# Regrouping the last stage of batch 0, splitting a table load, and moving three closing stores in a fused Fourier-filter and MLP kernel

## Chip, cores, metric

The kernel runs on one core of a Trainium2 chip. Times are device microseconds (us). "Time" is what is measured from outside; the profile's "span" runs from the first to the last instruction on the core and is about 1.8 us shorter. PE is TensorE's matmul stream, PEld its weight loads, DVE is VectorE, ACT ScalarE, POOL GpSimd, SP SyncE. An engine's name with a q is its sequencer.

## The reference

```python
# x: (8, 3008, 256)   filt_r, filt_i: (1505, 256)
X = np.fft.rfft(x, axis=1)
y = np.fft.irfft(X * (filt_r + 1j * filt_i)[None], n=3008, axis=1)
h = y.reshape(24064, 256) @ w_in                  # (256, 2048)
g = h + np.sin(alpha * h)**2 / (alpha + 1e-09)
out = g @ w_out                                   # (24064, 256), float32
```

## The kernel before

The Fourier transforms are done as small matmuls: 3008 points are 94 x 32, so each transform is one stage over 94 and one over 32. Batch 0 has a path of its own, kept in SBUF, on the chip; its last stage turns `t4_0` into `y`, the input of the hidden layer. Everything after that is a stream: for each chunk of 512 columns, 16 hidden blocks (two matmuls, a sine on ACT, a combination on DVE) and then the output projection, with the transforms of the next batches put between them at fixed slots.

Three places matter here. The first is the load of the inverse table `e_t`, in two halves on POOL's queue, each behind four loads of the filter:

```python
for g in range(2):
    gs = slice(12 * g, 12 * g + 12)
    for k, filt in enumerate((filt_r, filt_i)):
        for q in range(2):
            ...                                       # a quarter of this half of the filter
            nc.gpsimd.dma_start(out=f_t[k][64*k + 32*q : ..., gs, :], in_=...)
    nc.gpsimd.dma_start(out=e_t[:, gs, :], in_=e_dram.ap()[:, gs])
```

The second is the last stage of batch 0, in groups of four row columns. A pair of groups (one for each half of the channels) goes through a pool of two PSUM buffers, where the results of matmuls lie; ACT evacuates the first group (copies it to SBUF), DVE the second:

```python
def last(self, u, on_act=None):
    ch, rest = divmod(u, 4); half, cb = divmod(rest, 2)
    n0 = 8 * ch + 4 * half
    ps = fps.tile([128, 4, 128], FP32, tag="f")
    ...                                               # 4 x 2 matmuls into psv
    evac(y[:, cb, self.b % 2, n0:n0 + 4, :], psv, on_act)

def last_two(self, u):
    self.last(u, True)
    self.last(u + 1, False)
...
s0.last(0, True); s0.last(2, True); s0.last(1, True); s0.last(3, False)   # ahead of the hidden layer
for u in range(4, 16, 2):
    put((1, 3, 4.5, 6, 14, 16)[u // 2 - 2], s0.last_two, u, pe=True)      # inside the stream
```

The third is the output. A block of 128 rows is stored in runs, since rows of `out` lie 32 apart; each run is one DMA. All go to SP, except that the short second runs of the very last chunk go to POOL (first two tiles of 128 rows) and to ACT (last two tiles):

```python
store(o[:, i, :], pb, c0 + 128 * (t - t % 2 + i),
      nc.scalar if final else nc.gpsimd if k == len(chunks) - 1 else nc.sync)
```

## Time and profile before

| | before |
|---|---|
| time, median of the first 3 runs | 789.39 us (788.52 to 789.53) |
| span of the profiled run (its time: 790.81 us) | 789.0 us |
| first transpose of batch 0's inverse | 30.38 |
| first hidden block, from its second matmul (the first ran at 36.08) | 36.79 |
| end of the last matmul | 784.80 |
| SP's last store issued | 786.57 |

PE is busy 98% of the span. What the change touches is the first 55 us, where PE waits, and the 4.2 us after the last matmul. The lines that show this are in the prediction.

### The profile page before, as it was taken

Reading aid. Unit: us, or ns where it says so; the run is one execution under the profiler, and the core shown is the slowest. Engines: PE = TensorE matmul, PEld = TensorE weight load, DVE = VectorE, ACT = ScalarE, POOL = GpSimd, SP = SyncE. Lnnn points to the kernel's source line nnn. Section 1 sums busy time; section 2 is a strip of 40 time slices with the busy share of each in tenths; the row PEclk is TensorE's granted clock in tenths of the full one; section 3 lists DMA queues with packets and bytes.
Section 4 is the critical chain, followed back from the end, with each engine's and each line's share of the span. In section 5 each row is a group of like instructions: output and inputs, shape, how many; then the busy total and the mean of one; then the engine's idle time right before and its main releaser. Section 6 shows DMA issues by size and latency. Waiting matters only on the chain.

```text
span 789.0 us, 16730 instructions
## 1 busy us (share of the span) xinstructions
PE 776.2 (98%) x5854; PEld 536.3 (68%) x5854; DVE 657.4 (83%) x1171; ACT 617.0 (78%) x1209; POOL 79.7 (10%) x125
## 2 busy tenths in 40 slices
PE   8999989999999999999999999999999999999997
PEld 4756757676667766777666766777666776766666
DVE  7887987899878997799978998799987999777773
ACT  6887868888878887888887888788887887777663
POOL 6442000200020000200020000200002000000000
PEclk9999999999999999999999999999999999999999
DMA  9956568755573646554575455845566233421111
GB/s 217 257 105 173 118 144 206 173 104 134 140 198 82 135 98 191 150 121 102 121 210 124 100 106 137 219 94 113 128 165 171 62 97 82 116 62 29 41 41 54
DMA packets 87677, 101.01 MB, mean 128 GB/s; under 512 B 14472, under 2 KB 75928, under 8 KB 87592
## 3 DMA queue, kind: packets, MB, share of 16 engines
q1 hardware_dynamic: 78016, 73.73, 34.5%
q0 software_dynamic: 9360, 26.15, 17.4%
q8 instruction: 46, 0.75, 0.4%
q14 instruction: 39, 0.32, 0.1%
q10 hardware_dynamic: 216, 0.05, 0.0%
HBM read 55.72 MB, written 46.66 MB: 130 GB/s over the span
## 4 chain that ended last, share of the span: by engine, by line
PE 90%; DVE 2%; DMA 2%; ACT 2%; issue 1%; POOL 1%; SPq 1%; ACTq 0%; POOLq 0%; DVEq 0%
PE po L523 40%; PE ph L507 40%; PE pa L180 3%; PE pd L258 2%; PE pb L200 2%; PE pc L231 2%; DMA e_t<-e_tbl 1%; DVE v L511 1%; PE pd L255 1%; DMA xs<-xf 1%; ACT cos_all L510 1%; DVE t_h L385 1%; SPq L549 1%; ACT t_h L159 1%; DVE t_h L161 0%
## 5 line engine op out<-in xcount | busy, mean ns | idle before, releaser
L511 DVE SCALAR_TENSOR_TENSOR v<-cos_all,ph 128x512 f16<-128x512 f32 (+1 forms) x768 | 482.8, 671 | 107.4 <-ACT cos_all L510 103.9
L510 ACT ACTIVATE cos_all<-ph 128x512 f32<-128x512 f32 (+1 forms) x768 | 410.9, 592 | 99.5 <-PE ph L507 98.3
L523 PE MATMUL po<-w,v 128*128 128x256 f16 x3008 | 388.7, 272 | 0.0
L507 PE MATMUL ph<-y,w 128*128 128x512 f16 (+1 forms) x1536 | 386.4, 374 | 0.5 <-DVE y L161 0.3
L523 PEld LDWEIGHTS <-v 128*128 128x128 f16 x3008 | 289.3, 98 | 78.2 <-issue 1.2
L507 PEld LDWEIGHTS <-w 128*128 128x128 f16 x1536 | 147.5, 98 | 104.5 <-issue 2.5
L529 ACT COPY o<-po 128x512 f32<-128x512 f32 (+1 forms) x97 | 55.6, 573 | 19.6 <-PE po L523 12.6
L203 ACT CAST xf<-pb 128x512 f16<-128x512 f32 x84 | 50.0, 595 | 15.2 <-PE pb L200 13.8
L192 POOL DMA_DIRECT2D t<-d x56 | 36.3, 666 | 202.4 <-DMA out_dram<-o 128.6
L159 ACT CAST t_h<-pa 96x512 f16<-96x512 f32 x74 | 43.3, 586 | 8.5 <-PE pa L180 8.3
L140 POOL DMA_DIRECT2D x<-in_x_dram x32 | 17.1, 535 | 302.1 <-PE pc L231 171.4
L159 ACT CAST y<-pd 128x376 f16<-128x376 f32 x83 | 40.0, 482 | 7.6 <-PE pd L258 5.3
L258 PEld LDWEIGHTS <-t_h 96*128 96x128 f16 x448 | 31.4, 97 | 18.4 <-issue 0.4
L180 PE MATMUL pa<-x,wf_t 94*96 94x512 f16 x112 | 42.2, 381 | 1.0 <-DVE t_h L161 0.6
L159 ACT CAST g<-pc 128x512 f16<-128x512 f32 x58 | 34.4, 593 | 9.4 <-PE pc L231 9.0
L221 DVE TENSOR_TENSOR p<-p,xs 128x512 f16<-128x512 f16 x84 | 35.7, 425 | 2.9
L220 DVE TENSOR_TENSOR xs<-xs,filt_t 128x512 f16<-128x512 f16 x84 | 35.0, 416 | 2.8 <-DMA xs<-xf 2.8
L258 PE MATMUL pd<-wi_t,t_h 96*128 96x94 f16 x448 | 37.1, 204 | 0.0
L214 DVE TENSOR_TENSOR p<-xf,filt_t 128x512 f16<-128x512 f16 x84 | 35.0, 416 | 0.0
L231 PE MATMUL pc<-p,e_t 128*128 128x256 f16 x168 | 32.1, 273 | 1.7 <-DVE p L221 1.7
L200 PE MATMUL pb<-t,d_t 128*128 128x256 f16 x168 | 32.1, 272 | 0.5 <-DVE g L161 0.4
L161 DVE CAST t_h<-pa 96x512 f16<-96x512 f32 x38 | 25.9, 681 | 0.7 <-PE pa L180 0.5
(66 smaller groups left out, 257.5 us busy)
## 6 DMA issues: line engine op xcount, KB each, us to landing
x<-in_x_dram POOLq DMA_DIRECT2D x30, 376.0 KB, 5.0
d<-t_h SPq DMA_DIRECT2D x28, 384.0 KB
t<-d POOLq DMA_DIRECT2D x56, 192.0 KB, 4.6
xs<-xf SPq DMA_DIRECT2D x168, 64.0 KB
d<-g SPq DMA_DIRECT2D x56, 192.0 KB
t_h<-d SPq DMA_DIRECT2D x28, 384.0 KB
out_dram<-o SPq DMA_DIRECT2D x104, 80.0 KB
w_out<-in_moe_w_out_dram SPq DMA_DIRECT2D x1, 2048.0 KB
```

The source lines that it names most:

```text
L159: marks["act"] = nc.scalar.copy(out=dst, in_=src)
L180: marks["pe"] = nc.tensor.matmul(out=ps[0:NK, :], lhsT=wf_t, rhs=self.x[ch][:, 2 * j:2 * j + 2, :], start=True, stop=True)
L192: nc.gpsimd.dma_start(out=self.t2[g][64 * p:64 * p + 64, :, :], in_=self.d1[a0:a0 + 6, :, :].rearrange("s n c -> n s c"))
L200: nc.tensor.matmul(out=ps[:, i, :], lhsT=d_t[:, s, :], rhs=self.t2[s // 6][:, s % 6, :], start=True, stop=True)
L203: nc.scalar.copy(out=self.xf[u], in_=ps)
L231: nc.tensor.matmul(out=ps[:, i, :], lhsT=e_t[:, 2 * w + i, :], rhs=pt[:, i, :], start=(k == 0), stop=(k == len(pr) - 1))
L258: nc.tensor.matmul(out=psv[:, i, :], rhs=wi_t, start=True, stop=True, lhsT=t4_h[ch // 2][0:NK, n0 % 16 + i, cb * 128:cb * 128 + 128])
L507: nc.tensor.matmul(out=ps[:, 0:n], lhsT=w1[:, cb, jb * 128:jb * 128 + 128], rhs=y_cols[:, cb, c0:c0 + n], start=(cb == 0), stop=(cb == 1))
L510: nc.scalar.activation(out=cs[:, 0:n], in_=ps[:, 0:n], func=AFT.Sin, bias=float(np.pi / 2))
L511: marks["snake"] = nc.vector.scalar_tensor_tensor(out=v[k][:, jb, 0:n], in0=cs[:, 0:n], scalar=-1.0, in1=ps[:, 0:n], op0=ALU.add, op1=ALU. ...
L523: nc.tensor.matmul(out=pso[k][:, t % 2, :], lhsT=v[k][:, jb, 128 * t:128 * t + 128], rhs=w2[:, jb, :], start=(jb == 0), stop=(jb == 15))
L529: nc.scalar.copy(out=o[:, i0:t % 2 + 1, :], in_=pso[k][:, i0:t % 2 + 1, :])
```

## The change

Its intent: the first inverse matmuls waited for the table, so its first four classes are loaded apart, ahead of the filter's imaginary rows (A). The first hidden chunk needs only six row columns of the last stage, so the groups ahead of it have three each and the later ones five and four, and both groups of a pair go to one engine, the pairs alternating between DVE and ACT (B). And three more stores of the last chunk go from SP to POOL (C; not named in the change's title). Unused code that goes with it is cut.

```diff
+            if (g, k) == (0, 1):
+                nc.gpsimd.dma_start(out=e_t[:, 0:4, :], in_=e_dram.ap()[:, 0:4])
...
-        nc.gpsimd.dma_start(out=e_t[:, gs, :], in_=e_dram.ap()[:, gs])
+        es = slice(4 if g == 0 else 12, 12 * g + 12)
+        nc.gpsimd.dma_start(out=e_t[:, es, :], in_=e_dram.ap()[:, es])
...
+    def last_0(cb, n0, n1, on_act):
+        ...                                   # the same matmuls for row columns n0 to n1
+        evac(y[:, cb, 0, n0:n1, :], psv, on_act)
+    def last_two(i, n0, n1):
+        last_0(0, n0, n1, ([i % 2 == 1] * 2)[0])
+        last_0(1, n0, n1, ([i % 2 == 1] * 2)[1])
...
-    s0.last(0, True)
-    s0.last(2, True)
+    last_0(0, 0, 3, True)
+    last_0(0, 3, 6, True)
     warm_pe(3)
-    s0.last(1, True)
-    s0.last(3, False)
+    last_0(1, 0, 3, True)
+    last_0(1, 3, 6, False)
...
-                      nc.scalar if final else nc.gpsimd if k == len(chunks) - 1 else nc.sync)
+                      *(nc.sync, nc.scalar) if final else (nc.gpsimd if i else nc.sync, nc.gpsimd)
+                      if k == len(chunks) - 1 else (nc.sync, nc.sync))
...
-    for u in range(4, 16, 2):
-        put((1,3,4.5,6,14,16)[u // 2 - 2], s0.last_two, u, pe=True)
+    for i, n0 in enumerate((6, 11, 16, 20, 24, 28)):
+        put((1,3,4.5,6,14,16)[i], last_two, i, n0, (11, 16, 20, 24, 28, 32)[i], pe=True)
```

More of the change, by code (lines that the diff above doesn't have):

```diff
@@ L244, in load_t4, with last @@
                                in_=self.d2_rows[:, 8 * ch:8 * ch + 8, :])
-        def last(self, u, on_act=None):
+        def last(self, u):
             ch, rest = divmod(u, 4)
@@ L252, in last @@
             for i in range(4):
-                if self.b == 0:
-                    for k in range(2):
-                        nc.tensor.matmul(out=psv[64 * k:64 * k + 64, i, :], lhsT=t4_0[cb][:, n0 + i, :, k],
-                                         rhs=wi0_t, start=True, stop=True)
-                else:
-                    nc.tensor.matmul(out=psv[:, i, :], rhs=wi_t, start=True, stop=True,
-                                     lhsT=t4_h[ch // 2][0:NK, n0 % 16 + i, cb * 128:cb * 128 + 128])
-            evac(y[:, cb, self.b % 2, n0:n0 + 4, :], psv, on_act)
-        def last_two(self, u):
-            self.last(u, True)
-            self.last(u + 1, False)
+                nc.tensor.matmul(out=psv[:, i, :], rhs=wi_t, start=True, stop=True,
+                                 lhsT=t4_h[ch // 2][0:NK, n0 % 16 + i, cb * 128:cb * 128 + 128])
+            evac(y[:, cb, self.b % 2, n0:n0 + 4, :], psv)
     warm = cpool.tile([128, 1], FP32)
@@ L425, in inverse_0 @@
         evac(g_0[hc][:, 4 * w:4 * w + 4], ps.rearrange("p s (k c) -> p s c k", k=2), not (i in ()))
+    def last_0(cb, n0, n1, on_act):
+        ps = fps.tile([128, 4, 128], FP32, name=f"pd_0_{cb}_{n0}", tag="f")
+        psv = ps.rearrange("p a b -> p (a b)")[:, 0:(n1 - n0) * NR].rearrange("p (a r) -> p a r", r=NR)
+        for n in range(n0, n1):
+            for k in range(2):
+                nc.tensor.matmul(out=psv[64 * k:64 * k + 64, n - n0, :], lhsT=t4_0[cb][:, n, :, k],
+                                 rhs=wi0_t, start=True, stop=True)
+        evac(y[:, cb, 0, n0:n1, :], psv, on_act)
+    def last_two(i, n0, n1):
+        last_0(0, n0, n1, ([i % 2 == 1] * 2)[0])
+        last_0(1, n0, n1, ([i % 2 == 1] * 2)[1])
     w1 = cpool.tile([128, 2, DFF], FP16)
@@ L452, in weights_in @@
             after(ins, marks["products"])
-    s0 = Spectral(0)
     [inverse_table(g) for g in range(2)]
@@ L537, in runs, with store @@
         return [(0, whole), (whole, cnt - whole)] if 0 < whole < cnt else [(0, cnt)]
-    def store(o_blk, pb, col, second):
+    def store(o_blk, pb, col, *queues):
         p = 0
-        queues = [nc.sync, second]
         while p < 128:
```

## The prediction

> **What bounds the kernel now.** I read the page first, then the chain that ended last from 17 to 50 us, then the timeline of single engines there and over the last 11 us.
>
> ```profile
> span 789.0 us, 16730 instructions
> PE 776.2 (98%) x5854; PEld 536.3 (68%) x5854; DVE 657.4 (83%) x1171; ACT 617.0 (78%) x1209; POOL 79.7 (10%) x125
> ```
>
> PE is busy for 98%. The two large groups of matmuls are untouched, so the change can only win PE's idle time: at the start, in the first chunk, and after the last matmul. The chain shows the start (start us, us, what):
>
> ```profile
> 11.77 9.71 DMA e_t<-e_tbl
> 21.48 0.05 issue
> 21.53 0.64 PE pc L422 x8
> ...
> 30.38 4.51 DVE t_h L385 x2
> 34.89 0.04 issue
> 34.94 1.23 PE pd L255 x16
> 36.16 0.02 issue
> 36.19 0.56 DVE y L161
> 36.75 0.05 issue
> 36.79 0.82 PE ph L507 x3
> ```
>
> The first inverse matmuls wait until 21.48 for the inverse table; two transposes on DVE end at 34.89; 16 matmuls of the last stage and one evacuation then stand ahead of the first hidden block at 36.79. The timeline adds three things:
>
> ```profile
> 20.09 3.10 DVE L412 TENSOR_TENSOR p<-xf,filt_t 128x1024 f16<-128x1024 f16 x5
> 23.27 0.95 DVE L161 COPY filt_t<-filt_t 64x3072 f16<-64x3072 f16 x1
> 24.26 0.69 DVE L412 TENSOR_TENSOR p<-xf,filt_t 128x1024 f16<-128x1024 f16 x1
> 25.12 0.95 DVE L161 COPY filt_t<-filt_t 64x3072 f16<-64x3072 f16 x1 [0.17 <-DMA filt_t<-in_filt_i_dram]
> 26.21 3.70 DVE L412 TENSOR_TENSOR p<-xf,filt_t 128x1024 f16<-128x1024 f16 x6
> ```
>
> The first product is ready at 20.09 + 0.69 = 20.78, so the table costs 0.75 us there; but at 25.12 DVE waits for the second half of the filter, and the last six products follow that. In the first chunk:
>
> ```profile
> 45.01 0.68 PE L255 MATMUL pd<-wi_t,t_h 128*64 128x94 f16 x8 [0.56 <-ACT y L159]
> ```
>
> This is the second group of a pair. It waited for ACT's evacuation of the first group of the same pair (44.48 to 44.95): the two shared a buffer although the pool has two. At the end, the SP queue:
>
> ```profile
> 784.83 0.37 ACT L529 COPY o<-po 128x256 f32<-128x256 f32 x1 [1.38 <-DMA out_dram<-o]
> 783.71 1.33 SPq L549 DMA_DIRECT2D out_dram<-o  x3
> 785.77 0.80 SPq L549 DMA_DIRECT2D out_dram<-o  x2
> ```
>
> The last output tile is in SBUF at 785.20, but SP first issues its stores at 785.77 and ends at 786.57: it has issued without a wait since 778.46. It is late by its own queue.
>
> **What the Trainium skill says.** "DMA: Bandwidth & Descriptors", section "Issuing engines are not separate DMA queues": all issuers feed the same 16 DMA engines, and a second issuer saves only the sequencer's time. The tail agrees that this can matter: a store costs SP 0.31 to 0.68 us of issue. The same page, "Queues, rings and completion order": each DMA engine takes its descriptors in ring order. So a piece placed ahead of the filter arrives ahead of it, and all that follows has the same bytes in front of it as before. The trace agrees: the filter's four first-half loads (issued 5.0, 5.7, 8.57, 11.12) landed at about 15.5, 16.4, 17.3 and 18.3, the table at 21.48. "Perfetto Trace Analysis", section "Optimizing Scalar/DVE Operations": a fixed overhead per instruction, so larger ones pay. The trace agrees: on DVE 512 columns took 0.69 us and 376 took 0.54, thus 1.1 ns a column and some 0.13 us fixed; ACT 0.62 and 0.47. The number of evacuations stays 16, so this term is neutral.
>
> **Part A, table in three pieces.** The order of instructions built from the changed kernel shows the piece of 4 classes (128 KB) ninth on POOL, ahead of the imaginary filter. Each POOL DMA waits for the one eight before it, so waits shift by one: the first imaginary filter half waits for x2 (landed about 9.8) instead of x1 (8.57), and alpha's splitting behind it (2.1 us) ends near 12.5 instead of 11.17. The matmuls that spread alpha started at 12.17 and stood idle until the identity's landing afterwards (14.59), so 0.3 us is absorbed. The queue has 7 to 10 us of backlog, so later issues starve nothing. The piece lands near 17 (estimate: 16.4 plus 128 KB at 220 GB/s, 0.6 us). The imaginary filter moves back by the same 0.6, from 18.3 to 18.9, under 19.03, when DVE takes it up. The rest of the table lands at 21.5 as before, in time for the second inverse block, about 21.9. So the first inverse block starts at about 21.0 (the matmuls before it end at 20.99) instead of 21.53, and ACT, which idled 0.41 us before 22.19, evacuates it 0.41 earlier. That does not survive: inverse block 6 waited for DVE's product (27.05), and the products from 26.21 on depend on the filter's second half, which has the same bytes ahead of it. From there a product each 0.62, an evacuation each 0.62: I get the evacuation that releases the transposes ending at 30.2 instead of 30.35. A is worth 0.1 us, and could be -0.2 if that filter half lands later.
>
> **Part B, groups of 3, 5, 4.** The first hidden chunk needs 512 of 94 x 6 = 564 columns, so 6 row columns do, not 8. After the second transpose there are 12 matmuls, not 16: 4 x 1.23/16 = 0.31 us. The last evacuation has 282 columns: 0.55 - 94 x 1.1 ns = 0.45, 0.10 less. The first hidden block starts 0.41 + 0.1 earlier, at 36.3. But of the 8 matmuls that left the start 4 lay in the shade of a transpose and cost nothing, and all 8 come back in the first chunk, where the first two pairs have 20 instead of 16: 8 x 0.075 = 0.6 us of PE, half in each pair. The lead is 0.2 at the hidden pair of 39.84 and gone after the second pair. Then the pair on one engine pays: both groups of the third pair wait for ACT's evacuations of the pair before, done by 43.7, so the 0.56 us at 45.01 goes, and the hidden block of 45.62 starts near 45.1. From 46.26 to 54.6 ACT has hardly a gap (sines, two scalings, evacuations), and there it must now take two evacuations of the fourth pair instead of one: +0.40 at its pitch. ACT's lead of 0.6 falls to about 0.2, and PE, which has no gap from 49.9 to 58, then follows ACT's evacuation of the next batch's first stage. B with A's 0.1: 0.3 us. From there PE is without gaps for long stretches, so a lead is carried to the end.
>
> **Part C, stores of the last chunk** (not in the change's title). Three stores (8, 80, 26 rows: 0.36 + 0.44 + 0.42 = 1.22 us of issue) go from SP to POOL. SP then waits for its data instead: last tile at 785.20, 0.37 + 0.46 of issue, end 786.05 instead of 786.57. POOL has five stores from 782.21, 0.52 each: done at 784.8, landed 1.9 later, 786.7; not the end. C is worth 0.5 us.
>
> **Sum:** 0.1 + 0.2 + 0.5 = 0.8 us of 789.39, thus 788.6.
>
> **Rivals.** (1) The start's whole lead is carried: A 0.41, B 0.41, the removed wait 0.56, and C 0.5: 1.9 us, 787.5. For it speaks that each wait is on the chain; against it that DVE waits for the filter at 25.12, and that ACT is nearly full from 46.26. (2) The table's piece delays the filter: DVE's copy at 23.27 follows its landing (14.61 + 8.6 = 23.2) with nothing to spare, and 25.12 already waits. 0.3 us later there, with ACT's extra evacuation, eats B: only C is left, 788.9. (3) The tail does not shorten, as POOL's stores or the closing handshake end last: without C, 789.1. Against it: 1.9 us between POOL's landing and SP's.
>
> **Range and chances.** The three runs before span 1.0 us, and my terms are each uncertain by 0.2 to 0.4 us. I take 787.5 to 789.7 as eight in ten. 2% is 15.8 us, more than the span outside PE's busy time (12.8 us), so faster by 2% has no source; slower by 2% would need a matmul stretch at a lower clock, and the granted clock was 1.0 all along.
>
> **What would show each step.** A: first inverse matmuls near 21.0, no wait for the table there, the transposes near 30.2. If DVE shows a wait for the filter over 0.3 us before its copies, rival 2. B: 12 matmuls ahead of the first hidden block at about 36.3; no wait of a pd matmul for y in the first chunk; the first matmuls of the next batch's first stage (49.92 before) near 49.3, but their lead over before only 0.2 by 54. C: SP's queue with a wait for ACT before its last two issues, and its end some 1.3 us after the last matmul instead of 1.8. I am wrong if the matmul stream's last end (784.79) moves by over 0.8 us or not at all.

## The result, and the profile after

The changed kernel took 790.19 us (median of 4 runs, 789.22 to 791.39), against 789.43 (788.52 to 789.53) for the kernel before in the same rounds. The ratio is 1.0013, with a 95% interval from 0.9994 to 1.0032. Here and below a ratio is the mean time of one kernel's fast runs over the mean of the other's fast runs of the same rounds, so it is not quite the ratio of the medians. So the clock does not tell the two kernels apart in these rounds. The predicted 788.6 was too low, and the measured median lies above the stated range of 787.5 to 789.7.

The page of the changed kernel begins like this; PE's busy time is 0.9 us less than before, POOL's 2.2 more:

```profile
span 789.6 us, 16732 instructions
PE 775.3 (98%) x5854; PEld 536.1 (68%) x5854; DVE 657.0 (83%) x1171; ACT 616.4 (78%) x1209; POOL 81.9 (10%) x129
```

**First chunk.** PE's timeline after the change (start, busy time, engine, line, what; in brackets the idle time ahead of it and what ended it):

```profile
41.31 1.46 PE L427 MATMUL pd<-wi_t,t_h 128*64 128x94 f16 x20
43.67 1.23 PE L427 MATMUL pd<-wi_t,t_h 128*64 128x94 f16 x16
46.66 1.16 PE L427 MATMUL pd<-wi_t,t_h 128*64 128x94 f16 x16
49.14 0.38 PE L180 MATMUL pa<-x,wf_t 94*96 94x512 f16 x1 [0.34 <-ACT y L159]
52.79 0.38 PE L180 MATMUL pa<-x,wf_t 94*96 94x512 f16 x1 [0.21 <-ACT t_h L159]
```

All pairs now run as one piece of 20 or 16 matmuls; the gap of 0.56 us within the third pair is gone. In its place there is more waiting at the next batch's matmuls, whose first starts at 49.14 (49.92 before): the brackets are 0.34 and 0.21, where before only the first had one, of 0.26. Both waits are for ACT, which has one evacuation more to do here.

**Start.** DVE's timeline after the change:

```profile
19.26 0.95 DVE L161 COPY filt_t<-filt_t 64x3072 f16<-64x3072 f16 x1 [0.26 <-DMA filt_t<-in_filt_i_dram]
20.32 3.10 DVE L406 TENSOR_TENSOR p<-xf,filt_t 128x1024 f16<-128x1024 f16 x5
26.28 3.70 DVE L406 TENSOR_TENSOR p<-xf,filt_t 128x1024 f16<-128x1024 f16 x6
```

The first copy now waits 0.26 us for the filter's imaginary rows, behind which the piece of the table was put; the products start at 20.32, not at 20.09.

**End.** The copy of the last output tile by ACT, and the last DMA issues of SP and POOL in the changed kernel:

```profile
784.56 0.37 ACT L537 COPY o<-po 128x256 f32<-128x256 f32 x1 [1.37 <-PE po L531]
784.96 0.83 SPq L557 DMA_DIRECT2D out_dram<-o  x2
781.94 2.64 POOL L557 DMA_DIRECT2D out_dram<-o  x5 [181.87 <-ACT o L537]
```

SP now takes up the last tile's stores at 784.96, at once when the tile is there (784.93); before, it came 0.57 us late. That is what part C was for. But the closing DRAIN instructions tell another story. They stand on the line of kernel.py that opens and closes the kernel's tile context (L658 before, L666 after); on POOL, the trace shows one that lasts until some us after its last store. Each line has an engine's DRAINs of the kernel's end: how many, the shortest, median and longest in ns, and the starts of the first and the last. Before:

```profile
L658 POOLq DRAIN  x3: 46/98/4600, 782.6 to 788.7; - x3
L658 SPq DRAIN  x3: 7/7/7, 788.2 to 788.5; - x3
```

After:

```profile
L666 POOLq DRAIN  x3: 46/98/5122, 783.7 to 789.3; - x3
L666 SPq DRAIN  x3: 7/7/7, 787.6 to 789.1; - x3
```

POOL's first DRAIN starts just ahead of its last store's issue, and is the long one. Before it ran from 782.65 for 4.60 us, to 787.25, while SP reached its own at 788.19: POOL was ready first. After the change it ran from 783.71 for 5.12 us, to 788.83, while SP was ready at 787.61. SP was ready 0.58 us earlier (0.31 counted from the last matmul) and then waited for POOL. The view of waits of SP's queue over the last microseconds shows it. Before:

```profile
SPq L658 <- PEq L658: 0.7, 2, 0.5
```

After:

```profile
SPq L666 <- PEq L666: 1.8, 2, 1.4
```

The columns are the sum, the number and the longest of the waits. The engine named is PE's sequencer, but PE had been done for 3 us, so it stands for a later link of the closing handshake. The one that was late is POOL; the experiments test this.

In this pair of profiles, then, the last matmul ended 0.27 us earlier (784.80 and 784.53), and what follows it grew from 4.22 to 5.08 us: 0.86 us lost.

### The profile page after: what moved, and what is told of

It is laid out like the page before. It is cut to its first block, busy times and chain, and to the rows that moved or that the text cites. A ratio compares the mean times of both kernels' runs of the same rounds, so it can differ in the third digit from the quotient of the medians.

```text
span 789.6 us, 16732 instructions
## 1 busy us (share of the span) xinstructions
PE 775.3 (98%) x5854; PEld 536.1 (68%) x5854; DVE 657.0 (83%) x1171; ACT 616.4 (78%) x1209; POOL 81.9 (10%) x129
## 4 chain that ended last, share of the span: by engine, by line
PE 89%; DMA 4%; DVE 3%; ACT 2%; issue 1%; SPq 0%; POOL 0%; ACTq 0%; DVEq 0%; POOLq 0%
PE po L531 40%; PE ph L515 38%; PE pa L180 3%; PE pd L253 2%; PE pb L200 2%; PE pc L231 2%; DVE v L519 1%; ACT cos_all L518 1%; PE pd L427 1%; DMA d<-g 1%; DMA filt_t<-in_filt_i_dram 1%; DMA x<-in_x_dram 1%; DMA xs<-xf 1%; DVE t_h L379 1%; ACT t_h L159 1%
## 5 line engine op out<-in xcount | busy, mean ns | idle before, releaser
L159 ACT CAST y<-pd 128x376 f16<-128x376 f32 (+2 forms) x83 | 39.6, 480 | 7.7 <-PE pd L253 5.3
```

What stands on the lines that cost most here:

```text
L159: marks["act"] = nc.scalar.copy(out=dst, in_=src)
```

## The experiments

Each was run with five rounds beside the kernel before, four kernels to a chip. Since the time of one execution scatters by more than the whole change is worth, each profile is also measured against fixed points of its own trace:

- lead: from the start of the first transpose of batch 0's inverse to the start of hidden matmul number 40 (counted from 0, near 54 us). Part B is between these points, part A lies ahead of them.
- close: from the end of the last matmul to the end of the span. Part C is here.

| kernel | A, B, C | lead | close | median time | ratio, 95% |
|---|---|---|---|---|---|
| before | none | 24.12 | 4.22 | 789.43 | |
| changed | A B C | 23.87 | 5.08 | 790.19 | 1.0013 (0.9994 to 1.0032) |
| ab_only | A B | 23.80 | 4.61 | 790.52 | 1.0003 (0.9984 to 1.0023) |
| c_only | C | 24.17 | 5.08 | 790.14 | 1.0004 (0.9985 to 1.0023) |
| ab_act | A B, side stores on ACT | 23.86 | 4.19 | 790.07 | 0.9998 (0.9979 to 1.0017) |
| pool_all | A B, all seven on POOL | 23.86 | 6.28 | 790.96 | 1.0009 (0.9990 to 1.0028) |
| a_only | A | 24.06 | 3.71 | 790.24 | 1.0012 (0.9992 to 1.0031) |
| b_only | B | 23.91 | 4.77 | 788.82 | 0.9993 (0.9978 to 1.0008) |
| b_alt | A, B without the pairing | 24.16 | 4.03 | 789.01 | 0.9996 (0.9980 to 1.0012) |
| pool_prev | A B, POOL's stores earlier | 23.80 | 3.76 | 789.10 | 0.9992 (0.9977 to 1.0007) |
| before_again | none | 24.17 | 4.38 | 788.98 | 0.9987 (0.9967 to 1.0006) |
| after_again | A B C | 23.84 | 5.08 | 790.64 | 1.0011 (0.9990 to 1.0031) |
| pool_prev_again | as pool_prev | 23.81 | 3.77 | 789.29 | 0.9987 (0.9966 to 1.0008) |
| pool_tiny | A B, two late stores on POOL | 23.87 | 6.52 | 792.00 | 1.0024 (1.0003 to 1.0046) |

All gave correct results.

### First four: who loses at the end

Theory: C is the loss, by POOL's closing DRAIN. Rivals: A delays the filter and B's extra evacuations eat the lead; or the extra stores just load the DMA engines.

**ab_only**, the changed kernel with the store queues of the kernel before:

```diff
-  *(nc.sync, nc.scalar) if final else (nc.gpsimd if i else nc.sync, nc.gpsimd)
+  *(nc.sync, nc.scalar) if final else (nc.sync, nc.gpsimd)
```

> The changed kernel with the stores of the last chunk as they were before (three of them back from POOL to SP). Theory 1: the closing drain of POOL ends about 4.2 us after POOL's last store is issued (783.7 + 5.1 = 788.8 in the changed kernel, 787.2 before), and with five stores instead of two it, not SP, ends the program. Then this one has POOL's drain at about 787, SP last again, and is 0.2 to 0.4 us faster than before. Theory 2: the start (table in pieces, groups of 3 and 5) costs more than it gives: this one is as slow as the changed kernel, 0.5 to 1 us slower than before. Theory 3: the end of the matmuls is what it was and the difference is scatter between executions: no difference to before, and the same two clusters 1.9 us apart that the changed kernel's four runs show.

**c_only**, the kernel before with C alone:

```diff
-  nc.scalar if final else nc.gpsimd if k == len(chunks) - 1 else nc.sync)
+  *(nc.sync, nc.scalar) if final else (nc.gpsimd if i else nc.sync, nc.gpsimd)
+  if k == len(chunks) - 1 else (nc.sync, nc.sync))
```

> The kernel before with only the three stores moved from SP to POOL. Theory 1: POOL's stores start at 782.2, five times 0.53 us, drain 4.2 us later: 789.1 instead of SP's 788.25, so 0.6 to 0.9 us slower than before. Theory 2 (the start is the cause): 0.5 us faster than before, by SP's shorter queue. Theory 3: no difference.

**ab_act**, the changed kernel with the five side stores of the last chunk's first pair of tiles on ACT, none on POOL:

```diff
-  *(nc.sync, nc.scalar) if final else (nc.gpsimd if i else nc.sync, nc.gpsimd)
+  *(nc.sync, nc.scalar) if final else (nc.scalar if i else nc.sync, nc.scalar)
```

> The changed kernel with no store on POOL at all in the last chunk: ACT issues the five. Theory 1: POOL's drain is over long before, the end is SP's or ACT's last landing, near 787.6 minus: 0.8 to 1.2 us faster than before, the fastest of the four. ACT's issuing (five times 0.3 us) delays its next evacuation by up to 0.5 us, which should not reach the last tile. Theory 2: as slow as the changed kernel. Theory 3: no difference.

**pool_all**, with all seven stores of that pair on POOL:

```diff
-  *(nc.sync, nc.scalar) if final else (nc.gpsimd if i else nc.sync, nc.gpsimd)
+  *(nc.sync, nc.scalar) if final else (nc.gpsimd, nc.gpsimd)
```

> The changed kernel with all seven stores of the last chunk's first pair on POOL. Theory 1: two more stores put POOL's last issue 1.05 us later, its drain ends near 789.9: 0.8 to 1.1 us slower than the changed kernel, 1.2 to 1.9 slower than before. Theories 2 and 3: as the changed kernel or a little faster, as SP has less to issue.

Measured: c_only, with nothing but C, closes in 5.08 us, the same as the changed kernel to the hundredth. pool_all closes in 6.28: its last POOL store was issued 1.03 us later than in the changed kernel (1.09 against 0.06 us after the last matmul), and its close is 1.20 us longer. Its drain:

```profile
L666 POOLq DRAIN  x3: 46/98/5438, 788.8 to 794.7; - x3
```

The two kernels whose last POOL stores are early (ab_only) or gone (ab_act) close in 4.61 and 4.19 us. This fits the theory in order, but ab_only and ab_act were not shorter than the kernel before, and the clock tells none of the four from it. Two things made that so.

The first is SP. One of its stores, of 52 rows, which comes ahead of all stores of the last chunk, took 0.36 us to issue in some profiles and 1.27 to 1.81 in others, and in the latter SP is late at the end. So the close with the stores of the kernel before is a draw between 3.71 and 4.77 in six traces.

The second is that executions differ by more than that between 98 and 137 us. The waits of PE between 96 and 142 us, before:

```profile
PE pc L231 <- DVE p L221: 1.7, 2, 1.5
```

In the changed kernel:

```profile
PE pd L253 <- DMA t_h<-d: 1.7, 1, 1.7
PE pc L231 <- ACT xf L203: 1.1, 1, 1.1
```

In c_only:

```profile
PE pc L231 <- ACT xf L203: 0.7, 1, 0.7
```

This is batch 1's chain through DRAM, where PE waits for transfers once here and once there. From hidden matmul 120 to number 192 the traces took 37.5 us (ab_only, b_only, c_only, ab_act, pool_prev_again) to 39.8 (b_alt), with no order by A, B or C. pool_all's profile took 41.8, but that has in part another cause: its run, of 796.79 us against 790.34 to 791.80 for its other six, shows the TensorE clock granted at half in two stretches of 3.4 us, at 22.8 to 26.2 and at 132.0 to 135.4 us. Both lie ahead of the close, which is what is read from it. The rest adds next to no scatter: all 14 traces took 43.72 to 43.77 us from hidden matmul 40 to number 120, and 647.01 to 647.04 from number 192 to the last matmul.

### Second four: A, B and the halves of B

**a_only**, the kernel before with the table in three pieces (the first two parts of the change's diff and nothing else).

> The kernel before with part A alone (the table in three pieces). Theory: A is worth nothing beyond the scatter of the start: first transpose somewhere between 30.1 and 31.2 us (before 30.38, kernel with C alone 30.24, after 30.23), first transpose to the 40th hidden start 24.1 us as before (24.12 and 24.17 without B), last matmul to the end of the span 4.2 to 4.6 us, time ratio 1.000 within 0.002. Rival, my step A: 0.1 us earlier. Rival 2 of the prediction: the piece of the table delays the imaginary filter rows, first transpose 0.2 us later and the time 0.2 us longer; then the wait for the filter's imaginary rows on VectorE must show again (0.26 us in the changed kernel) and the first transpose come later than in the runs without A.

**b_only**, the kernel before with the new groups and pairs, the table in two halves and the stores as they were.

> The kernel before with part B alone (groups of 5 and 4 row columns, a pair on one engine). Theory: first transpose to the 40th hidden start 23.85 us (23.80 to 23.87 in the four kernels with A and B, 24.12 and 24.17 in the two without B), so B alone carries the 0.28 us; first transpose to the first matmul of the next batch 18.9 us against 19.55; closing part as in the kernel before, 4.2 to 4.6 us. Ratio 0.9996, not to be told from 1 by the clock. Rival: the 0.28 us come from A and B together (the pair's first products lie earlier because the table is there earlier), then 24.0 to 24.2 here.

**b_alt**, A and B with the old stores, but a pair shared by the two engines again:

```diff
-        last_0(0, n0, n1, ([i % 2 == 1] * 2)[0])
-        last_0(1, n0, n1, ([i % 2 == 1] * 2)[1])
+        last_0(0, n0, n1, True)
+        last_0(1, n0, n1, False)
```

> A and B with the stores of the kernel before, but in each pair the first group is evacuated by ScalarE and the second by VectorE. Tells apart the two halves of B. If the gain is from one engine taking a pair (theory: the second group of a pair waited for the other, later engine), the wait for ScalarE's evacuation of y, about half a microsecond, is back before a group of the third or a later pair, and first transpose to the 40th hidden start is 24.05 to 24.2. If the gain is from the group sizes alone, it is 23.85 as with A and B, and there is no such wait. Closing part 4.2 to 4.6 us in both.

Measured: the lead is 24.06 with A alone and 23.91 with B alone, so B carries it. In b_alt it is back at 24.16, and the wait of the kernel before is back with it, to the same 0.56 us:

```profile
45.27 0.67 PE L427 MATMUL pd<-wi_t,t_h 128*64 128x94 f16 x8 [0.56 <-ACT y L159]
```

So the gain needs the pairing; the group sizes without it win nothing by 54 us. The pairing with the old group sizes was not run. Over all traces, the lead was 24.06 to 24.17 in the five with the engines mixed within a pair (before, c_only, a_only, before_again, b_alt) and 23.80 to 23.91 in the nine with the pairing. The means are 24.14 and 23.85, a gain of 0.29 us. By the steady 43.72 to 43.77 us that follow, it is carried to hidden matmul 120; behind that the scatter of 2.3 us hides it, and the clock does not show B either (b_only: 0.9993, interval up to 1.0008).

A trades one wait for another. In a_only DVE's copy waited for the filter as in the changed kernel; in c_only, which has no A, it didn't, and the transposes came no later. a_only:

```profile
19.45 0.96 DVE L161 COPY filt_t<-filt_t 64x3072 f16<-64x3072 f16 x1 [0.35 <-DMA filt_t<-in_filt_i_dram]
30.40 2.31 DVE L388 STREAM_TRANSPOSE t_h<-t_h 128x2048 uint32<-128x2048 uint32 x1 [0.26 <-ACT t_h L159]
```

c_only:

```profile
19.29 0.96 DVE L161 COPY filt_t<-filt_t 64x3072 f16<-64x3072 f16 x1
30.24 2.31 DVE L385 STREAM_TRANSPOSE t_h<-t_h 128x2048 uint32<-128x2048 uint32 x1 [0.26 <-ACT t_h L159]
```

In both, the transpose starts 10.95 us after that copy: DVE's products and copies between them run back to back, and the table plays no part. In the first profile of the kernel before the table had come last; in c_only and b_only the chain that ended last went through the input `x` instead, and in a_only through the filter's imaginary rows.

Over all traces: without A the first inverse matmul waited for the table in two of four, starting 0.75 us (before) and 1.24 us (before_again) after its product was ready. With A it started within 0.1 us of its product in all ten. But the imaginary rows that this copy needs landed (the later of two loads) at 18.09 to 19.21 without A (mean 18.49) and at 18.59 to 20.71 with it (mean 19.38), and the copy waited 0.26 to 1.02 us for them in eight of the ten traces with A, at most 0.15 in the four without. The first transpose started at 29.87 to 31.14 in the four traces without A (mean 30.41) and at 29.78 to 32.32 in the ten with it (mean 30.58, or 30.39 without pool_all). So no net gain or loss of A is shown.

### The drain, earlier and later

**pool_prev**, A and B with POOL's stores moved to where they have time: three stores of the chunk before the last go to POOL, the last chunk's go to SP and ACT.

```diff
-  *(nc.sync, nc.scalar) if final else (nc.gpsimd if i else nc.sync, nc.gpsimd)
-  if k == len(chunks) - 1 else (nc.sync, nc.sync))
+  *(nc.sync, nc.scalar) if k == len(chunks) - 1 else
+  (nc.gpsimd, nc.gpsimd) if k == len(chunks) - 2 and t == 3 and i else (nc.sync, nc.sync))
```

> A and B; the three stores of the second block of the last tile of the chunk before the last (64, 12 and 52 rows) go to GpSimd, and all stores of the last chunk to SyncE and ScalarE. Theory (GpSimd's closing drain ends 4.0 to 4.4 us after its last store is issued, whatever else runs): GpSimd's drain ends near the last matmul, at least 2 us before SyncE's, SyncE is not late with the last chunk's stores, and last matmul to the end of the span is 3.7 to 4.1 us, against 4.22 before and 5.08 after; ratio 0.999. Rival (the close is long whenever GpSimd has stores late in the kernel, or SyncE takes longer for the last chunk's seven stores): 4.6 us or more, with SyncE's last store issued 1.8 us or more after the last matmul.

**pool_tiny**, A and B with two small stores of the very last tile (2 and 14 rows) on POOL, all else on SP and ACT:

```diff
-  *(nc.sync, nc.scalar) if final else (nc.gpsimd if i else nc.sync, nc.gpsimd)
-  if k == len(chunks) - 1 else (nc.sync, nc.sync))
+  *(nc.sync, nc.gpsimd if t == 3 else nc.scalar) if k == len(chunks) - 1 else
+  (nc.sync, nc.sync))
```

> A and B; GpSimd gets two stores only, of 2 and 14 rows, of the very last tile (number and size almost as in the kernel before, 6 and 14 rows, but about 3 us later); all others on SyncE and ScalarE. Theory (GpSimd's drain ends 4.0 us after its last store is issued, no matter how few they are): last store issued 1.5 us after the last matmul, drain over at 5.5, end of the span 6.2 to 6.4 us after the last matmul, and the time over 1.5 us longer than that of the version with the early stores. Rival (the drain grows with the number or the bytes of GpSimd's stores: five in the changed kernel, seven in the slowest): two small stores are drained quickly and the closing part is 3.7 to 4.8 us.

**before_again**, **after_again** and **pool_prev_again** are the three kernels once more.

> The kernel before once more, as a run of its own against itself: what the clock makes of no change at all. Ratio 1.000 within 0.0015 either way; single times from 788 to 792.5 us. Last matmul to the end of the span between 3.7 and 4.8 us, as in the five kernels with the same closing stores (3.71, 4.03, 4.22, 4.61, 4.77), with GpSimd's drain over about 4.0 us after its last store and before SyncE's.

> The changed kernel once more. Theory (A 0, B -0.28, C +0.8 us): last matmul to the end of the span 5.08 us again, since GpSimd's drain is tied to its last store and not to SyncE's state; first transpose to the 40th hidden start 23.85 us; pooled with the first measurement 0.3 to 0.8 us slower than before. Rival: the 5.08 us of the first profile was one draw of the same scatter as before's 3.7 to 4.8, then another value here and a ratio below 1.

> The version with GpSimd's stores taken from the chunk before the last, once more. Theory: last matmul to end 3.76 us again (0.5 less than before's mean 4.27, and without its scatter, 1.3 less than after), B's 0.28 kept, so 0.8 us under before and 1.6 under after in the mean: ratio to before 0.9990, to the changed kernel in the same rounds 0.998. Rival: 3.76 was a lucky draw, then 4.2 to 4.8.

Measured, in us from the end of the last matmul of the same trace:

| kernel | stores of POOL at the end | POOL's last store issued | POOL's DRAIN over | SP's last store issued | span's end |
|---|---|---|---|---|---|
| pool_prev | 3 | -4.44 | -0.36 | 1.25 | 3.76 |
| pool_prev_again | 3 | -4.45 | -0.37 | 1.26 | 3.77 |
| a_only | 2 | -1.54 | 2.46 | 1.26 | 3.71 |
| b_alt | 2 | -1.54 | 2.45 | 1.59 | 4.03 |
| before | 2 | -1.55 | 2.45 | 1.77 | 4.22 |
| before_again | 2 | -1.54 | 2.46 | 1.93 | 4.38 |
| ab_only | 2 | -1.53 | 2.46 | 2.16 | 4.61 |
| b_only | 2 | -1.55 | 2.45 | 2.32 | 4.77 |
| c_only | 5 | 0.06 | 4.30 | 1.27 | 5.08 |
| changed | 5 | 0.06 | 4.30 | 1.26 | 5.08 |
| after_again | 5 | 0.06 | 4.30 | 1.27 | 5.08 |
| pool_all | 7 | 1.09 | 5.50 | 1.26 | 6.28 |
| pool_tiny | 2 | 1.74 | 5.73 | 1.84 | 6.52 |

ab_act is left out, as its POOL has no store there. POOL's DRAIN ends 3.99 to 4.41 us after the issue of its last store, in all thirteen traces. Two stores give 4.0, seven give 4.4; how late the last one is counts far more than how many there are. This holds for these stores of 2 to 80 KB and not for every DMA: in ab_act POOL's last DMAs were loads of 192 KB, and its DRAIN ended at 607.2, 8.5 us after the last issue. pool_tiny is the sharpest case: the same number and nearly the same bytes as before, 3.3 us later, and the longest close of all. Its drain, beside that of pool_prev. pool_tiny:

```profile
L666 POOLq DRAIN  x3: 46/98/4598, 785.1 to 790.2; - x3
L666 SPq DRAIN  x3: 7/7/7, 787.5 to 789.9; - x3
```

pool_prev:

```profile
L666 POOLq DRAIN  x3: 46/97/4817, 778.4 to 787.1; - x3
L666 SPq DRAIN  x3: 7/7/7, 786.5 to 786.9; - x3
```

The drain of pool_prev is even a little longer than that of pool_tiny, but it starts at 778.4 and is over before the last matmul. The table falls into two kinds. In the first eight rows the end follows SP's last store by 2.44 to 2.51 us; in the last five it follows POOL's DRAIN by 0.78 or 0.79. So in these traces the close is the later of the two:

close = max(SP's last issue + 2.45, POOL's last issue + about 4.2 + 0.78).

My expectation for pool_tiny, 6.2 to 6.4, was 0.1 to 0.3 too low because POOL issued its first store 0.26 us later than ACT had issued the same one (0.70 and 0.44 us after the last matmul). pool_prev met its expectation of the close, and again in its repetition. after_again closed in 5.08 us as expected.

By the clock: the changed kernel, its repetition and c_only, all with C, have 16 runs of mean 790.58 us. The kernel before (43 runs in all), a_only, b_only, b_alt and ab_only, all with the old stores, have 67 runs of mean 789.70. The difference is 0.88 us with a standard error of 0.30 (if anything too small, since 10 of the 16 also have B's pairing and 12 of the 67); the traces give 5.08 less the mean close of six, 4.29, thus 0.79. pool_prev has 12 runs of mean 789.06: 1.62 us (standard error 0.45) less than the changed kernel's 10 runs of mean 790.68, where the traces give 5.08 - 3.77 = 1.31. Against the kernel before, 789.68 over 43 runs, pool_prev is 0.62 us less with a standard error of 0.35; the traces give 0.29 + 4.29 - 3.77 = 0.81. By the traces it is the best version found (b_only's median, 788.82, is lower still, within the noise), but on the clock alone its lead over the kernel before is not certain. The runs that are pooled here come from several calls, on chips 0, 6 and 15 for the experiments; within one call no ratio to the kernel before but pool_tiny's leaves 1. The last call, however, held three of the kernels side by side, six runs each: there after_again was 1.85 us slower than pool_prev_again (standard error 0.67), and pool_tiny 2.98 (0.59), where the traces' closes give 1.31 and 2.75.

before_again is the measure of the clock itself: the same kernel against itself, five rounds, gave 0.9987, as much as the change was ever expected to bring. Its expectation (1.000 within 0.0015) held just so.

What stays open: why SP's 52-row store needs 0.36 us in some executions and up to 1.81 in others. It was short in all traces with C and in pool_tiny, but also in a_only and b_alt, which have the old stores, and it is issued ahead of every store that C moves. One hint: in the five traces where it is long, it ended 0.27 to 0.39 us after a 16 KB packet of the instruction queue (q8) that began near its start; but the short traces have such a packet near it too.

## Why the prediction was wrong

**Part C failed.** The step reads: "POOL has five stores from 782.21, 0.52 each: done at 784.8, landed 1.9 later, 786.7; not the end. C is worth 0.5 us." The half about SP was right: SP waited for its data, and ended 1.26 us after the last matmul (1.3 said; 1.84 in the mean of the six traces with the old stores). But the 0.5 us to be won there was a matter of the draw: the prediction gave a store 0.31 to 0.68 us of SP's issue and passed over the one that took 1.27 in the profile it read; in a_only, with the old stores and that one short, SP ended at the same 1.26. The half about POOL took the landing of the stores as POOL's end. The last of them landed at 785.89, but POOL's own closing DRAIN ran on to 788.83, 2.94 us after it, and the closing handshake waits for that. C therefore costs 0.79 us (traces) or 0.88 (clock) instead of winning 0.5, a difference of 1.3 us or so. The profile before could have told it: the 4600 ns on POOL's sequencer ended 0.94 us ahead of SP's DRAIN, so C had 0.94 us of room on POOL and moved POOL's last store by 1.61. Rival 3 named the place ("POOL's stores or the closing handshake end last") and was set aside with the landing as the argument; it also called this case 789.1, "without C", as if the tail could only stay.

**Part A shows no gain, where 0.1 was said.** Its marks held in the profile of the changed kernel: inverse matmuls at 21.07 (21.0 said), transposes at 30.23 (30.2 said), no wait for the table. But c_only shows the same 30.24 without A, so meeting the mark was luck. And rival 2's wait was there: 0.26 us, just under the 0.3 that I had set as its sign, and over 0.3 in seven of the ten traces with A, 0.57 in the changed kernel's repetition. The prediction let the imaginary rows land 0.6 us later, "under 19.03"; in the two profiles they landed 0.83 later (18.34 and 19.17). That loads on POOL's queue land in the order of their issue is here the trace's word (15.72, 16.70, 17.34, 18.25, 19.17 in the changed kernel): the section that the prediction cites ("DMA: Bandwidth & Descriptors", "Queues, rings and completion order") says of SP's and ACT's rings that descriptors are consumed in order, not that they complete in order.

**Part B was right.** 12 matmuls ahead of the first hidden block, whose second matmul (the mark used above) started at 36.26 (36.3 said); no wait of a last-stage matmul for `y` in the first chunk; the next batch's first matmul at 49.14 (49.3 said), with the lead mostly given back to ACT. 0.29 us by 54 us, in place of 0.2.

**The sum.** With the terms read from the traces it is 0 + 0.29 - 0.79: the kernel is 0.5 us slower, where I had 0.8 faster. The clock has 1.0 us slower with a standard error of 0.4 (10 runs against 43), so the sign is clearer than the size.

**The range was too narrow as well.** It rested on "The three runs before span 1.0 us". The 43 runs of the kernel before span 787.72 to 793.00, with a standard deviation of 1.32 us and a mean of 789.68: the kernel before itself falls above my upper end of 789.7 nearly half the time. That the time would stay within 2% held.

## What to carry to other kernels

When a store is moved to another engine to relieve a queue at the very end, follow that engine to its own closing DRAIN, not to the landing of its data: on GpSimd here the DRAIN was over about 4.2 us after its last store's issue, so in this kernel GpSimd may store early and must stop early. When two work pieces share a pair of buffers and one of two engines is late, try giving a whole pair to one engine: here that took away a 0.56 us wait, for the price of another evacuation on ACT. A wait that is removed can come back behind another load, so look at what was moved back as well (part A). And before a change of 0.1% is judged by the clock, measure the kernel against itself, and use intervals within the trace between marks that the scatter doesn't touch.

## What the Trainium skill lacked or had wrong

- "VectorE: DVE Perf Modes", section "The DRAIN you can't avoid", tells of two kinds of DRAIN: the one after each VectorE operation, and the runtime's own at a kernel's beginning and end, about 12 ns, constant, on all engines. It lacks the ones that matter here, which stand on the kernel's own line that closes its tile context: SP's are 7 ns, but the first of POOL's three is 4598 to 5438 ns in the kernels where GpSimd has issued stores near the end, and it sets the end of the kernel when they are late.
- "DMA: Bandwidth & Descriptors", section "Anatomy of one DMA — SWDGE (gpsimd) path", gives a fixed cost of about 2.0 us for a DMA from GpSimd. POOL's late stores here landed 1.7 to 2.1 us after the start of their issue, which agrees; but the section has nothing on the close, in which GpSimd is busy 2.94 us beyond the landing of its last store (785.89 to 788.83 in the changed kernel).
- "Perfetto Trace Analysis", section "DMA Instruction — SWDGE (GPSIMD)", says that the profile's end of such an instruction is the end of descriptor generation and not of the movement. The runs agree: 0.53 us in the profile, landing 1.84 us after the start for the last one. It lacks that the engine's end isn't the landing either.
- No page that I found tells how far the single times of one kernel scatter: 788 to 793 us over 43 runs here, at a granted clock of 0.99 to 1.0. The traces show it at the start, between 98 and 137 us, and in SP's last stores.
